# One queue slot earlier for half of one quad's attention weights, in a fused memory-attention and token-mixer kernel

## The chip, the cores and the metric

The kernel runs on one core of one Trainium2 chip. The metric is the device time of one execution in microseconds (us). Three runs of the kernel before gave 792.73, 793.41 and 793.94 us, a median of 793.41 us. PE is the matrix engine (TensorE; PEld its weight loads), DVE the vector engine, ACT the scalar engine, POOL is GpSimd, and SP is the engine whose queue issues the transfers.

## The reference

Eight batches, eight heads, 576 positions, head size 64, 32 memory slots. A softmax of `phi` pools keys and values into 32 slots per head, each query attends to these slots, and the result goes through a token mixer (576 to 256 to 576) and a channel mixer (512 to 1536 to 512), each with a residual:

```python
a = exp(phi - max(phi, axis=2)); a = a / (sum(a, axis=2) + 1e-9)   # over the 576 positions
k_m, v_m = einsum('bhsm,bhsd->bhmd', a, k), einsum('bhsm,bhsd->bhmd', a, v)
attn = softmax(q @ k_m^T / 8)                                       # over the 32 slots
x = (attn @ v_m) laid out as (batch, 576, 512)
u = x + (relu(x^T @ w_tok1) @ w_tok2)^T
out = u + relu(u @ w_ch1) @ w_ch2
```

Everything is float32. The kernel splits each operand of the large products into a high part in a rounded format (fp32r) and a low part, the rest, and adds three products, high by high, high by low and low by high.

## The kernel before

**Tiles and stages.** The four heads of half a batch are a *quad*; `Quad(b, Q)` names it by batch and half, so (2, 0) is the third batch's first quad. The channel mixer works on nine *chunks* of 512 of the 8 x 576 rows. A chunk has twelve pairs of products: the first (`cp`, line 159, twelve matmuls of 128x512) gives a block of 128 hidden channels, which ACT cuts at zero into a high part `hh` (line 126) and DVE completes with the low part `hl` (line 129); the second (`acc`, line 192, twelve matmuls) adds that block's part of the output. In the stage that matters here PE does `cp` of the next block and then `acc` of the block before it, over and over, and the attention of later batches is slipped in between.

**One quad's steps.** `load_phi`; `phi_max` (DVE reduces to `pr`, line 259, then POOL's all-partition maximum `prr`, line 270); `phi_exp` (DVE subtracts, line 273, ACT exponentiates, line 283); `phi_sum` (DVE line 259, POOL's all-partition sum `psr`, line 292); `step_kv` (`kvp`); `step_s` (scores `sp`); `sm2`, the softmax, whose end `sm3` sends the weights out and back by DMA as `raw`, transposes them into the tile `aT` and calls `a_pair(0)`; `a_pair(1)`; `nat` (`raw` into high and low parts); `v_pairs` (`vv`, line 484); `step_A` (`Ap`, then its parts `Ah` on ACT and `Al` on DVE); `step_R` (`Rp`, line 552, whose first matmul needs `Ah` and whose third needs `Al`); and `step_u` (`u`, line 573).

**The step that moves.** `a_pair(p)`, line 471, takes one half (64 of 128 partitions) of `aT`: ACT copies it to a high part (line 475), POOL subtracts for the low part (line 476). `v_pairs` puts its result `vv` in the same storage as `aT` (one buffer), so its first ACT copy cannot start before POOL has read the second half of `aT`. On ACT these stand behind each other: `vv`, `uh` (a chunk's left-over rows), `hh`, `Ah`.

**What sets the order.** Up to the end of chunk 0 a planner orders the steps. From there a table of events does: `at(h, fn, argument, k)` puts a call in slot h, sub-slot k (0 where none is given). For product number g the loop issues `cp` of g, then `run(2g-1, 1)`, then `hh` and `hl` of g, then `run(2g, 0)`, `acc` of the product before, `run(2g, 1)`, and `run(2g+1, -1, 0)`. Calls of one slot are issued in the order in which they were entered. The quad (2, 0), named `second`, has r = 24, so `sm2` stands in slot 27; the next quad, (2, 1), has its `phi_max` in slot 27 with k = 1, which the loop runs after slot 27's k = 0. Instructions of one engine run in the order in which they were issued.

POOL's `tensor_tensor` and its all-partition reductions run from different code libraries. Where one kind follows the other, the program holds an instruction between them that changes the library, shown as a bare `ISA` row in the listings below and as a `MODIFY_POOL_CONFIG` of POOL's queue in the trace.

Of the kernel before, what the change touches and what calls it, by code (L numbers as in the profile page):

```python
# [28 lines left out]
def kernel(  # L29
# [192 lines left out]
    def mixer(c):  # L222
        if c not in chunks:
            chunks[c] = Chunk(c)
        return chunks[c]
# [1033 lines left out]
    for Q, h0 in ((0, 3), (1, 11)):  # L1259
        qd = quads[1, Q]  # L1260
# [9 lines left out]
    second = ThirdBatchQuad(2, 0)  # L1270
# [34 lines left out]
    def at(h, fn, *x, k=0):  # L1305
        events.setdefault((max(h, 0), k), []).append((fn, x))

    beside = {}
    for b in range(2, B):
        for Q in range(2):  # L1310
            qd = second if b == 2 and not Q else Quad(b, Q)
            r = 2 * NF * b - (14 if Q else 26)
            if b == 2 and not Q:
                r = m = 2 * NF
            else:

                m = r - (0 if b == 2 else 10 if b > 3 or Q else 8)
                at(max(m - 11, 2 * NF), qd.load_phi)
                at(m - (6 if (b, Q) == (3, 0) else 7), qd.phi_max, k=1)
                at(m - 4, qd.phi_exp, k=1)  # L1320
                at(m - 3, qd.phi_sum, k=1)
                at(loaded + 1, qd.load_kv, k=1)
                at(r - 4, qd.load_q, k=1)
            loaded = m
            at(m, qd.step_kv)
            at(m + 4, qd.values)
            if b > 2:
                at(m + 3, qd.get_keys, k=1)
            else:
                at(m + 1, qd.step_T)  # L1330
            at(r + 2, qd.step_s)
            if Q or b == 2:
                at(r + 3, qd.sm2)
            else:
                beside[r + 3] = qd
            at(r + 4, qd.a_pair, 1)
            at(r + 6, qd.nat, k=1)
            at(r + 7, qd.v_pairs)
            at(r + 8, qd.step_A)
            at(r + 9, qd.step_R)  # L1340
            for x in range(4):
                at(r + 10 + x // 2 * (1 if qd is second else 2), qd.step_u, x // 2, x % 2)
        at(2 * NF * (b - 1) + 7, lambda b=b: mixer(b).take(), k=1)
    for c in range(CHUNKS):
# [6 lines left out]
        if h + 1 in beside:  # L1351
            qd = beside.pop(h + 1)
# [120 lines left out]
```

## Time and profile before

| what | number |
|---|---|
| median of 3 runs | 793.41 us (792.73 to 793.94) |
| the profiled execution's own time | 793.46 us |
| its span, first to last instruction | 791.6 us |
| PE busy | 765.9 us, 97% of the span |
| PEld busy | 638.3 us, 81% |
| DVE busy | 367.7 us, 46% |
| ACT busy | 246.4 us, 31% |
| POOL busy | 144.1 us, 18% |
| mean granted PE clock | 0.991 of full speed |

The span starts at 0 and all positions are in us from there; 1.86 us of the execution's time lie outside it. A row of a timeline gives the start, the duration, the engine, the line, the operation, output from input, the shape, the count, and in brackets how long the engine sat idle before and what ended it. Matmuls overlap: one is shown as lasting 0.39 us while the next starts 0.23 us after it. The changed lines are run once each, near 160 us of the 791.6.

### The profile page before, as it was taken

Reading aid. Unit: us, or ns where it says so; the run is one execution under the profiler, and the core shown is the slowest. Engines: PE = TensorE matmul, PEld = TensorE weight load, DVE = VectorE, ACT = ScalarE, POOL = GpSimd, SP = SyncE. Lnnn points to the kernel's source line nnn. Section 1 sums busy time; section 2 is a strip of 40 time slices with the busy share of each in tenths; the row PEclk is TensorE's granted clock in tenths of the full one; section 3 lists DMA queues with packets and bytes.
Section 4 is the critical chain, followed back from the end, with each engine's and each line's share of the span. In section 5 each row is a group of like instructions: output and inputs, shape, how many; then the busy total and the mean of one; then the engine's idle time right before and its main releaser. Section 6 shows DMA issues by size and latency. Waiting matters only on the chain.

```text
span 791.6 us, 11381 instructions
## 1 busy us (share of the span) xinstructions
PE 765.9 (97%) x4651; PEld 638.3 (81%) x4651; DVE 367.7 (46%) x640; ACT 246.4 (31%) x470; POOL 144.1 (18%) x124
## 2 busy tenths in 40 slices
PE   6799999978999999999999999999999999999998
PEld 5687878767787878788878888888878788888887
DVE  5989874434636444544344443536262422212113
ACT  3797664122322222232314232333233220210110
POOL 1344223010231013110221013101310402002000
PEclk9999999997999999999999999999999999999999
DMA  9916330141412312150406040504030101001001
GB/s 333 419 50 219 155 148 25 68 129 67 108 42 68 135 35 114 17 185 12 137 2 199 2 148 2 182 20 148 1 92 28 31 1 53 1 1 53 1 1 53
DMA packets 52243, 68.95 MB, mean 87 GB/s; under 512 B 33632, under 2 KB 42848, under 8 KB 47584
## 3 DMA queue, kind: packets, MB, share of 16 engines
q1 hardware_dynamic: 51616, 67.71, 25.6%
q8 instruction: 36, 0.59, 0.3%
q10 hardware_dynamic: 576, 0.52, 0.2%
q14 instruction: 15, 0.12, 0.1%
HBM read 54.92 MB, written 13.30 MB: 86 GB/s over the span
## 4 chain that ended last, share of the span: by engine, by line
PE 80%; DVE 10%; DMA 5%; issue 2%; ACT 2%; SPq 0%; POOL 0%; DVEq 0%; ACTq 0%; POOLq 0%
PE cp L159 34%; PE acc L192 32%; PE u L573 7%; DMA rawc<-in_w_ch_dram 3%; PE Ap L533 3%; DMA raww<-in_w_tok_tail_dram 2%; PE Rp L552 1%; DVE o L210 1%; PE end L192 1%; PE kvp L305 1%; DVE rawc L638 1%; DVE S L435 1%; DVE sm L430 1%; DVE S L411 1%; PE kvp L936 1%
## 5 line engine op out<-in xcount | busy, mean ns | idle before, releaser
L192 PE MATMUL acc<-hh,c 128*128 128x512 f32 x832 | 277.6, 394 | 0.8
L129 DVE SCALAR_TENSOR_TENSOR hl<-cp,hh 128x512 fp32r<-128x512 f32 x104 | 71.7, 690 | 278.9 <-ACT hh L126 278.8
L192 PEld LDWEIGHTS acc<-hh,c 128*128 128x128 f32 x832 | 156.2, 188 | 40.6 <-issue 6.5
L159 PE MATMUL cp<-uh,c1h 128*128 128x512 f32 x432 | 164.4, 394 | 0.0
L159 PE MATMUL cp<-ul,c1h 128*128 128x512 f32 x432 | 163.4, 392 | 0.0
L159 PE MATMUL cp<-uh,c1l 128*128 128x512 f32 x432 | 163.0, 391 | 0.0
L192 PE MATMUL acc<-hl,c 128*128 128x512 f32 x416 | 162.3, 390 | 0.0
L126 ACT ACTIVATE hh<-cp 128x512 fp32r<-128x512 f32 x104 | 62.0, 596 | 274.6 <-PE cp L159 274.6
L159 PEld LDWEIGHTS cp<-uh,c1l 128*128 128x128 f32 x432 | 81.6, 189 | 17.3
L159 PEld LDWEIGHTS cp<-ul,c1h 128*128 128x128 f32 x432 | 81.7, 189 | 16.6
L159 PEld LDWEIGHTS cp<-uh,c1h 128*128 128x128 f32 x432 | 81.1, 189 | 16.8 <-issue 0.4
L192 PEld LDWEIGHTS acc<-hl,c 128*128 128x128 f32 x416 | 78.2, 188 | 13.9
L476 POOL TENSOR_TENSOR a<-aT,a 64x576 fp32r<-64x576 f32 x24 | 34.3, 1428 | 217.8 <-ACT a L475 116.6
L204 POOL TENSOR_TENSOR o<-uh,ul 128x512 f32<-128x512 f32 x36 | 48.7, 1382 | 114.3 <-PE cp L159 46.9
L259 DVE TENSOR_REDUCE pr<-phi 128x128 f32<-128x640 f32 x27 | 35.4, 1315 | 15.2 <-ACT phi L283 8.1
L573 PE MATMUL u<-w2h,Rl 128*128 128x288 f32 x128 | 37.8, 295 | 0.2 <-DVE Rl L129 0.2
L573 PE MATMUL u<-w2l,Rh 128*128 128x288 f32 x128 | 37.8, 295 | 0.0
L573 PE MATMUL u<-w2h,Rh 128*128 128x288 f32 x128 | 37.7, 295 | 0.0
L475 ACT CAST a<-aT 64x576 fp32r<-64x576 f32 x24 | 16.2, 673 | 56.0 <-DVE aT L441 55.7
L533 PE MATMUL Ap<-w1h,nat 128*128 128x256 f32 x144 | 28.7, 291 | 0.7 <-DVE nat L983 0.7
L129 DVE SCALAR_TENSOR_TENSOR Rl<-Rp,Rh 128x512 fp32r<-128x512 f32 x16 | 11.1, 691 | 36.2 <-ACT Rh L126 36.2
L292 POOL PARTITION_ALL_REDUCE psr<-pr x11 | 11.9, 1082 | 73.8 <-issue 47.7
(156 smaller groups left out, 893.6 us busy)
## 6 DMA issues: line engine op xcount, KB each, us to landing
kv<-in_kv_dram SPq DMA_DIRECT2D x15, 1280.0 KB, 6.9
rawc<-in_w_ch_dram SPq DMA_DIRECT2D x12, 1024.0 KB, 9.8
q<-in_q_dram SPq DMA_DIRECT2D x16, 576.0 KB, 5.6
out_dram<-o SPq DMA_DIRECT2D x8, 1024.0 KB, 7.4
phi<-in_phi_dram SPq DMA_DIRECT2D x16, 320.0 KB, 4.1
rows<-S SPq DMA_DIRECT2D x48, 72.0 KB, 2.0
raw<-rows SPq DMA_DIRECT2D x12, 256.0 KB, 2.9
kv<-in_kv_dram SPq DMA_DIRECT2D x2, 640.0 KB, 12.1
```

The lines of the kernel that those rows point to most:

```text
L126: nc.scalar.activation(out=h, in_=ps, func=AF.Relu)
L129: nc.vector.scalar_tensor_tensor(out=l, in0=ps, scalar=0.0, in1=f32(h), op0=ALU.max, op1=ALU.subtract)
L159: nc.tensor.matmul(ps, l[:, a, w], r[:, a], start=n == 0, stop=n == len(mm) - 1)
L192: nc.tensor.matmul(ps, l_[f // 2][:, f % 2, a * P : (a + 1) * P], r[:, w], start=f == start and x == 0, stop=f == end - 1 and x == 2,)
L204: nc.gpsimd.tensor_tensor(out=s.o[:, a], in0=f32(s.uh[:, a]), in1=f32(s.ul[:, a]), op=ALU.add)
L210: nc.vector.tensor_tensor(out=o, in0=ps or s.acc[a], in1=o, op=ALU.add)
L259: nc.vector.tensor_reduce(out=m.rearrange("p (i m) -> p i m", i=4), in_=s.pt.rearrange("p i j m -> p i m j"), axis=AX.X, op=op,)
L292: nc.gpsimd.partition_all_reduce(s.r, m, P, RED.add)
L475: nc.scalar.copy(out=h, in_=s.aT[own])
L476: nc.gpsimd.tensor_tensor(out=l, in0=s.aT[own], in1=f32(h), op=ALU.subtract)
L533: nc.tensor.matmul(ps[:, :TT], a, w, start=x == 0, stop=x == len(mm) - 1)
L573: nc.tensor.matmul(ps[:, :HALF], a, r, start=x == 0, stop=x == len(mm) - 1)
```

## The change

`a_pair(1)` of the third batch's first quad goes from slot r + 4 to slot r + 3; all other quads keep r + 4. In slot r + 3 it stands directly behind `sm2`, which ends with `a_pair(0)`. It so comes ahead of `phi_max` of quad (2, 1) and ahead of `hh` and `hl` of the product in between.

```diff
@@ -1333,7 +1333,7 @@
                 at(r + 3, qd.sm2)
             else:
                 beside[r + 3] = qd
-            at(r + 4, qd.a_pair, 1)
+            at(r + (3 if qd is second else 4), qd.a_pair, 1)
             at(r + 6, qd.nat, k=1)
             at(r + 7, qd.v_pairs)
             at(r + 8, qd.step_A)
```

POOL's queue, from the residual of chunk 0 (`o`) to the sum of quad (2, 1). `a_2_0_1598` and `a_2_0_1599` are the two halves' tiles; the number behind `prr` and `pr` counts tiles and shifts by two:

```order
 L204 TENSOR_TENSOR o_1341<-uh_556,ul_557 128x512 x4
 L476 TENSOR_TENSOR a_2_0_1598<-aT_0_1596,a_2_0_1598 64x576
+L476 TENSOR_TENSOR a_2_0_1599<-aT_0_1596,a_2_0_1599 64x576
 L270 ISA
-L270 ISA prr_1_1619<-pr_1_1617 128x128
-L476 ISA
-L476 TENSOR_TENSOR a_2_0_1599<-aT_0_1596,a_2_0_1599 64x576
-L292 ISA
+L270 ISA prr_1_1621<-pr_1_1619 128x128
 L292 ISA psr_1_1702<-pr_1_1700 128x128
```

The second half's subtraction moves ahead of the maximum of the next quad. With it go two of the bare `ISA` rows, the one ahead of the second half (L476) and the one ahead of the sum (L292); POOL has two instructions fewer and all others as before.

ACT's queue, from the exponential of quad (2, 0)'s scores (`S`) to that of the next quad's `phi`:

```order
 L426 ACTIVATE S_0_1560<-S_0_1560 128x576
 L475 CAST a_2_0_1598<-aT_0_1596 64x576
-L126 ACTIVATE hh_1_1622<-cp_1_1604 128x512
-L350 CAST vh_0_1626<-vb_0_1507 128x256
 L475 CAST a_2_0_1599<-aT_0_1596 64x576
+L126 ACTIVATE hh_1_1624<-cp_1_1606 128x512
+L350 CAST vh_0_1628<-vb_0_1507 128x256
 L126 ACTIVATE hh_1_1657<-cp_1_1644 128x512
 L122 CAST nat_0_1673<-raw_0_1593 128x512
 L122 CAST nat_0_1673<-raw_0_1593 64x128
 L283 ACTIVATE phi_1_1509<-phi_1_1509 128x640
```

The second copy moves ahead of one `hh` and one `vh` copy, which each come one copy later. DVE, PE and SP keep their order, but for the numbers of tiles.

## The prediction

> **What bounds the kernel now.** I began with PE's busy share in the page, 97%, then asked the waits of PE, longest first. This is the first of them:
>
> ```profile
> PE 765.9 (97%) x4651; PEld 638.3 (81%) x4651; DVE 367.7 (46%) x640; ACT 246.4 (31%) x470; POOL 144.1 (18%) x124
> PE Rp L552 <- ACT Ah L122: 6.3, 1, 6.3
> ```
>
> PE is the bound, and in one place it stands for 6.3 us because `Ah` is late. The timelines of PE, ACT and POOL there say why:
>
> ```profile
> 173.55 0.39 PE L192 MATMUL acc<-hh,c 128*128 128x512 f32 x1
> 180.19 0.58 PE L552 MATMUL Rp<-vh,Ah 128*128 128x256 f32 x1 [6.26 <-ACT Ah L122]
> 181.10 0.58 PE L552 MATMUL Rp<-vh,Al 128*128 128x256 f32 x1
> 182.12 0.63 PE L159 MATMUL cp<-uh,c1h 128*128 128x512 f32 x1
> ...
> 169.30 0.74 ACT L283 ACTIVATE phi<-phi 128x640 f32<-128x640 f32 x1 [3.10 <-DVE phi L273]
> 177.54 1.22 ACT L484 CAST vv<-vh 64x128 fp32r<-64x128 f32 x4 [7.50 <-POOL a L476]
> 179.78 0.36 ACT L122 CAST Ah<-Ap 128x256 fp32r<-128x256 f32 x1
> ...
> 160.46 1.42 POOL L476 TENSOR_TENSOR a<-aT,a 64x576 fp32r<-64x576 f32 x1 [26.63 <-issue]
> 167.68 0.72 POOL L270 PARTITION_ALL_REDUCE prr<-pr  x1 [5.80 <-DVE nat L123]
> 176.12 1.39 POOL L476 TENSOR_TENSOR a<-aT,a 64x576 fp32r<-64x576 f32 x1 [7.71 <-issue]
> 183.32 1.09 POOL L292 PARTITION_ALL_REDUCE psr<-pr  x1 [5.82 <-PE Rp L552]
> ```
>
> POOL is idle 5.80, 7.71 and 5.82 us between a subtraction and a reduction: the changes of library. The second half waits for two of them, `vv` on ACT waits 7.50 us for it, `Ah` stands behind `vv`, and PE behind `Ah`. PE also comes back slowly. The chain shows the product behind the wait and a usual one, and the stretches of time show the clock (PEclk, behind the busy times; the last two columns are DMA share and GB/s):
>
> ```profile
> 182.32 4.91 PE cp L159 x12
> 214.58 2.72 PE cp L159 x12
> ...
> 26.41:29.82 3.41, 1.01 (x10) 0.82 (x9) 3.27 (x7) 2.82 (x5) 1.49 (x1) 1.00 1.02 420
> 29.82:33.23 3.41, 3.41 (x17) 3.18 (x17) 3.06 (x6) 3.41 (x6) 1.09 (x1) 0.50 1.00 406
> 50.30:53.71 3.41, 1.99 (x16) 1.80 (x15) 3.41 (x8) 3.06 (x6) 2.31 (x1) 1.00 0.00 0
> 173.18:176.59 3.41, 0.75 (x4) 0.29 (x2) 0.00 (x0) 0.00 (x0) 0.47 (x1) 1.00 0.00 0
> 176.59:186.83 10.24, 6.53 (x18) 5.17 (x19) 3.50 (x5) 3.16 (x8) 2.71 (x3) 0.50 0.00 0
> ```
>
> The clock fell to 0.50 for 10.24 us behind a stretch with PE busy 0.75 of 3.41 us, and earlier for 3.41 us behind one with 1.01; a stretch with 1.99 left it at 1.00. So the wait costs its own length and 4.91 - 2.72 = 2.19 us on the next product.
>
> **The change part by part.** *The second half.* It now follows the first on POOL. Such a pair takes 2.99 us in the next quad:
>
> ```profile
> 206.86 2.99 POOL L476 TENSOR_TENSOR a<-aT,a 64x576 fp32r<-64x576 f32 x2 [7.99 <-ACT a L475]
> 217.16 0.72 POOL L270 PARTITION_ALL_REDUCE prr<-pr  x1 [7.30 <-issue]
> 302.23 0.72 POOL L270 PARTITION_ALL_REDUCE prr<-pr  x1 [7.48 <-DMA kv<-in_kv_dram]
> 349.57 0.72 POOL L270 PARTITION_ALL_REDUCE prr<-pr  x1 [11.31 <-DVE Rl L129]
> 385.26 0.72 POOL L270 PARTITION_ALL_REDUCE prr<-pr  x1 [6.91 <-DMA kv<-in_kv_dram]
> 468.36 0.72 POOL L270 PARTITION_ALL_REDUCE prr<-pr  x1 [6.38 <-DVE pr L259]
> 553.05 0.72 POOL L270 PARTITION_ALL_REDUCE prr<-pr  x1 [7.47 <-DMA kv<-in_kv_dram]
> ```
>
> It ends at 160.46 + 2.99 = 163.45. The 7.71 us change of library is gone from the path of `vv`, and so is the 5.82 us one ahead of `psr`, which nobody waited for.
>
> *What is late next.* `vv` then no longer waits for POOL, but ACT still does the next quad's exponential ahead of it, and that waits for `prr`. `prr` needs one change of library, which now starts at 163.45 instead of 160.46 + 1.42 = 161.88. Before, the exponential ended at 169.30 + 0.74 = 170.04, which is 2.36 us after `prr` began. So `vv` starts at 163.45 + R + 2.36 = 165.81 + R, where R is the length of that change.
>
> *What R is.* Here before it was 5.80 us, and 5.82 us for `psr`. Where the queue had large loads in flight it was longer, as the rows above show: 7.30, 7.48, 6.91, 6.38 and 7.47, and at the longest 11.31. Starting later, it moves into such a load:
>
> ```profile
> 161.88:167.68 5.80, 5.80 (x27) 4.83 (x26) 1.96 (x4) 1.42 (x3) 0.00 (x1) 1.00 0.61 169
> 163.42:170.53 7.11, 7.11 (x37) 6.06 (x37) 2.95 (x5) 2.16 (x4) 0.72 (x1) 1.00 0.89 303
> 294.75:302.23 7.48, 7.48 (x41) 6.43 (x40) 3.97 (x6) 3.51 (x9) 0.00 (x1) 1.00 0.93 320
> 177.51:183.32 5.81, 3.02 (x9) 2.52 (x10) 3.14 (x5) 3.16 (x8) 0.00 (x0) 0.50 0.00 0
> 163.54 0.54 SPq L236 DMA_DIRECT2D phi<-in_phi_dram  x1
> 164.13 0.42 SPq L213 DMA_DIRECT2D out_dram<-o  x1
> ```
>
> The DMA engines were busy 0.61 of the old change and 0.89 of the time that the new one would take, near the 0.93 of the 7.48 us row. Neither `phi` nor the store moves. I take the mean of those five rows, (7.30 + 7.48 + 6.91 + 6.38 + 7.47) / 5 = 7.11 us, with 5.80 and 11.31 as bounds. The rows cannot tell whether a store delays it as a load does.
>
> The Trainium skill (GPSIMD Engine Reference, 2.1 Instruction dispatch) budgets about 6 us, 5.95 measured, for the first call after a library is loaded, whatever else runs. The trace agrees where the queue is empty (5.82) and not where it is busy (up to 11.31). By 5.95 the sum below would be 1.16 us larger.
>
> *PE.* `vv` starts at 165.81 + 7.11 = 172.92, 4.62 us earlier than 177.54. `uh`, `hh`, `Ah` and `Al` follow it as before, so `Rp` starts 180.19 - 177.54 = 2.65 us behind it at 175.57, and its third matmul 181.10 - 177.54 = 3.56 us behind at 176.48. At full clock `cp` follows that third matmul by 222.27 - 221.79 = 0.48 us:
>
> ```profile
> 221.79 0.28 PE L552 MATMUL Rp<-vh,Al 128*128 128x256 f32 x1
> 222.27 0.40 PE L159 MATMUL cp<-uh,c1h 128*128 128x512 f32 x1
> ```
>
> `cp` starts at 176.96 instead of 182.12: 5.16 us. PE is free at 173.55 + 0.23 = 173.78, so it still waits 1.79 us for `Ah` and, after 0.24 us of work, 0.67 us for `Al`. If the clock stays full, the product behind it saves 2.19 us.
>
> *What the moved copy delays.* ACT's second copy now stands ahead of `hh`, which comes one copy later, 160.24 - 159.66 = 0.58 us:
>
> ```profile
> 159.66 0.67 ACT L475 CAST a<-aT 64x576 fp32r<-64x576 f32 x1 [2.94 <-DVE aT L441]
> 160.24 0.59 ACT L126 ACTIVATE hh<-cp 128x512 fp32r<-128x512 f32 x1
> 160.86 0.69 DVE L129 SCALAR_TENSOR_TENSOR hl<-cp,hh 128x512 fp32r<-128x512 f32 x1
> 163.91 0.39 PE L192 MATMUL acc<-hh,c 128*128 128x512 f32 x1
> ```
>
> `hl` ends near 162.1 instead of 161.55, and `acc` needs it at 163.91: 1.8 us of cover, cost nothing. Without cover it would be 0.58 us. The low part of `v`, next on DVE, may wait for POOL until 163.45 and is first needed by `Rp`. The two library changes taken away cost nobody else: `psr` comes earlier. SP's order does not change.
>
> *Sum.* 5.16 + 2.19 = 7.35 us. Against the profiled execution's 793.46 that is 786.1 us; that execution stands 0.05 us over the median. Everything behind moves up together, since PE is busy from there to the end. If PE waited for nothing here, `cp` would start at 173.78 + 0.71 = 174.49 and the gain would be 9.82 us, the ceiling.
>
> **The rivals.** *The change of library is not stretched.* For it: the same place took 5.80 us with the first of these transfers in flight. `cp` then starts 1.31 us earlier: 784.8 us. By the skill's 5.95 it would be 784.9, and the same happens.
>
> *The clock falls all the same.* PE's two waits are 2.46 us together, so a stretch of 3.41 us that holds both has 0.95 us of work, which lies between the two rows that were followed by 0.50. A stretch that holds one of them has more. Where those stretches begin against the program is nothing I can set. It costs from half of 3.41 us, 1.7, to the 2.7 that the slow products cost before (2.19, and 182.12 - 181.10 - 0.48 = 0.54): 787.8 to 788.8.
>
> The Trainium skill (TensorE: Matmul & The Clock Gate, Part 1: The HAM clock gate) lets the clock fall after an idle window of about 3.4 us. The two rows with 1.01 and 0.75 us of work in it show that the window need not be quite idle. By the page alone a wait of 2.46 us keeps the full clock and 786.1 stands.
>
> *The change of library takes as long as the longest row.* With 11.31 us `vv` starts at 177.12, 0.42 before now, and the clock falls as before: 793.0, no change. Against it: in that row's place a load of keys and values and a store are both in flight; here only the store is.
>
> *Slower.* `vv` comes later than now if R exceeds 177.54 - 165.81 = 11.73 us, and each us more costs one. If the code waits for the store and for `q` behind it, half as much stretch again as in the longest row, R = 11.31 + (11.31 - 5.80) / 2 = 14.07, gives 793.46 + 2.34 = 795.8. No row is that long.
>
> *The move hides nothing.* POOL's order could keep `vv` waiting for another reason; the 7.50 us row names the second half alone.
>
> **How the numbers follow.** Chances: forecast, R of 6.4 to 7.5 at full clock, 0.42; not stretched 0.25; clock falls 0.23; longest row 0.05; slower 0.02; the move does nothing 0.03. The three cases that gain give 784.8, 786.1 and 787.8 to 788.8; the range from 784.5 to 788.8 holds them, with 0.1 left out. 0.2% is 1.6 us, about what a measurement can tell here. Faster 0.90, within 0.2% 0.08, slower 0.02.
>
> **What would show it.** On POOL two subtractions follow each other near 160.5 and `psr` follows without 5.8 us idle. ACT's wait of 7.50 us for POOL is gone, and `vv` starts with the end of the exponential, near 172.9. `Rp` waits about 1.8 us for `Ah` and the product behind it takes 2.7 us. It is wrong if the idle time ahead of `prr` exceeds 8 us, if that product takes 4 us or more, or if a new wait of PE appears at 163.9.

## The result, and the profile after

The changed kernel takes 785.09 us, the median of four runs (784.90 to 785.84); the kernel before takes 793.07 us (four runs, 792.16 to 793.94). The ratio is 0.9901, with a 95% interval of 0.9884 to 0.9918. The median fell by 7.98 us where 7.35 were forecast, and the time lies 1.0 us under the forecast and inside the range. The profiled execution took 785.84 us, the longest of the four; its span is 784.1 us.

The page's busy times, and the waits of PE from 155 to 180 us, after the change; they answer to the first two rows of the prediction:

```profile
PE 763.5 (97%) x4651; PEld 637.0 (81%) x4651; DVE 366.7 (47%) x640; ACT 247.8 (32%) x470; POOL 144.3 (18%) x124
```

```profile
PE Rp L552 <- ACT Ah L122: 1.1, 1, 1.1
PE Rp L552 <- DVE Al L123: 0.5, 1, 0.5
```

The wait for `Ah` is 1.1 us instead of 6.3, there is a small one for `Al`, and PE has no other in this stretch. The timeline of the same place after the change, POOL, ACT, DVE and PE in turn:

```profile
159.06 2.93 POOL L476 TENSOR_TENSOR a<-aT,a 64x576 fp32r<-64x576 f32 x2 [26.63 <-issue]
168.66 0.72 POOL L270 PARTITION_ALL_REDUCE prr<-pr  x1 [6.67 <-issue]
172.55 1.08 POOL L292 PARTITION_ALL_REDUCE psr<-pr  x1 [3.17 <-DVE pr L259]
...
158.25 1.38 ACT L475 CAST a<-aT 64x576 fp32r<-64x576 f32 x2 [2.94 <-DVE aT L441]
159.65 0.60 ACT L126 ACTIVATE hh<-cp 128x512 fp32r<-128x512 f32 x1
170.27 0.74 ACT L283 ACTIVATE phi<-phi 128x640 f32<-128x640 f32 x1 [5.72 <-DVE phi L273]
170.92 1.21 ACT L484 CAST vv<-vh 64x128 fp32r<-64x128 f32 x4
...
160.89 1.38 DVE L354 TENSOR_TENSOR vl<-vb,vh 128x256 fp32r<-128x256 f32 x1
...
172.13 0.39 PE L192 MATMUL acc<-hh,c 128*128 128x512 f32 x1
173.57 0.39 PE L552 MATMUL Rp<-vh,Ah 128*128 128x256 f32 x1 [1.05 <-ACT Ah L122]
174.61 0.45 PE L552 MATMUL Rp<-vh,Al 128*128 128x256 f32 x1 [0.53 <-DVE Al L123]
175.50 0.63 PE L159 MATMUL cp<-uh,c1h 128*128 128x512 f32 x1
```

The two subtractions now run as one pair; one change of library (6.67 us) is left ahead of `prr`; `psr` follows with no change of library; `vv` starts with the end of the exponential and waits for POOL no more. This execution reached the stage 1.41 us earlier than the one profiled before, since ACT's first copy starts at 158.25 instead of 159.66. That lead came about ahead of the changed place, and I take it off: `cp` starts at 175.50 instead of 182.12, which is 6.62 - 1.41 = 5.21 us earlier. The chain of waits and the stretches of time (PEclk behind the busy times) show the product behind it:

```profile
175.70 3.98 PE cp L159 x12
```

```profile
171.38:174.79 3.41, 1.83 (x9) 1.08 (x8) 2.99 (x5) 2.11 (x6) 1.08 (x1) 1.00 0.00 0
174.79:178.21 3.42, 3.42 (x11) 2.84 (x12) 1.63 (x2) 0.60 (x1) 0.70 (x1) 0.50 0.00 0
178.21:181.62 3.41, 3.41 (x23) 3.08 (x21) 1.11 (x2) 1.00 (x2) 0.00 (x0) 1.00 0.03 7
```

Here the clock still fell, for one stretch of 3.42 us instead of 10.24, and the product took 3.98 us instead of 4.91: 0.93 us saved where 2.19 were forecast. The gain between the two profiled executions is 5.21 + 0.93 + 1.41 = 7.55 of the measured 7.62 us, of which 6.14 belong to the change.

### The profile page after: what moved, and what is told of

Same layout as the page of the kernel before. It is cut to its first block, busy times and chain, and to the rows that moved or that the text cites. A ratio compares the mean times of both kernels' runs of the same rounds, so it can differ in the third digit from the quotient of the medians.

```text
span 784.1 us, 11378 instructions
## 1 busy us (share of the span) xinstructions
PE 763.5 (97%) x4651; PEld 637.0 (81%) x4651; DVE 366.7 (47%) x640; ACT 247.8 (32%) x470; POOL 144.3 (18%) x124
## 4 chain that ended last, share of the span: by engine, by line
PE 79%; DVE 10%; issue 6%; DMA 2%; ACT 1%; POOL 1%; SPq 0%; DVEq 0%; ACTq 0%; POOLq 0%
PE cp L159 33%; PE acc L192 31%; PE u L573 7%; PE Ap L533 3%; DMA kv<-in_kv_dram 1%; PE Rp L552 1%; DVE o L210 1%; DMA rawc<-in_w_ch_dram 1%; PE end L192 1%; PE kvp L305 1%; DVE rawc L638 1%; DVE S L411 1%; PE kvp L936 1%; DVE S L435 1%; DVE mx L418 1%
## 5 line engine op out<-in xcount | busy, mean ns | idle before, releaser
L476 POOL TENSOR_TENSOR a<-aT,a 64x576 fp32r<-64x576 f32 x24 | 34.3, 1431 | 209.5 <-ACT a L475 116.6
L292 POOL PARTITION_ALL_REDUCE psr<-pr x11 | 11.9, 1083 | 72.3 <-issue 48.1
```

Of the source, the lines that this page charges most:

```text
L292: nc.gpsimd.partition_all_reduce(s.r, m, P, RED.add)
L476: nc.gpsimd.tensor_tensor(out=l, in0=s.aT[own], in1=f32(h), op=ALU.subtract)
```

## The experiments

Theory: what cost the time was the change of library between the two halves, on the path from the second half over `vv` and `Ah` to `Rp`; the slow clock behind the wait was a cost of its own; and what is late next is `prr`, through the exponential that stands ahead of `vv`. The rivals: the place of ACT's copy was the cause; or the slow clock costs nothing; or something on POOL other than the change of library. Line numbers differ by a few between these kernels, since some add lines. The diffs of the first three runs are against the kernel before, the others against the changed kernel.

**1. The copy alone.** ACT's copy of the second half moves as in the change; POOL's subtraction stays where it was.

```diff
-        def a_pair(s, p):
+        def a_pair(s, p, parts=(0, 1), eng=None):
...
-            nc.scalar.copy(out=h, in_=s.aT[own])
-            nc.gpsimd.tensor_tensor(out=l, in0=s.aT[own], in1=f32(h), op=ALU.subtract)
+            if 0 in parts:
+                nc.scalar.copy(out=h, in_=s.aT[own])
+            if 1 in parts:
+                (eng or nc.gpsimd).tensor_tensor(out=l, in0=s.aT[own], in1=f32(h), op=ALU.subtract)
...
-            at(r + 4, qd.a_pair, 1)
+            if qd is second:
+                at(r + 3, qd.a_pair, 1, (0,))
+            at(r + 4, qd.a_pair, 1, (1,) if qd is second else (0, 1))
```

> Only ACT's copy of the second half moves up, as in the change; POOL's subtraction stays behind the next quad's maximum. If the gain comes from POOL's library changes (theory), nothing is gained: POOL still changes library twice more, ACT's vv still waits about 7.5 us and PE about 6.3 us for Ah, ratio 1.000 within 0.002. If it comes from ACT's new order (rival), most of the 1% gain is here: ratio 0.990 to 0.993.

Measured: 791.93 us against 792.90, ratio 0.9991 [0.9973, 1.0009]. The waits of PE, and the timeline of POOL and ACT:

```profile
PE Rp L554 <- ACT Ah L122: 5.9, 1, 5.9
```

```profile
174.96 1.39 POOL L478 TENSOR_TENSOR a<-aT,a 64x576 fp32r<-64x576 f32 x1 [7.54 <-issue]
176.38 1.22 ACT L486 CAST vv<-vh 64x128 fp32r<-64x128 f32 x4 [7.32 <-POOL a L478]
```

`vv` still waits 7.32 us for POOL's second half. The interval cannot tell the copy's gain from zero, so the change's gain lies with POOL's subtraction.

**2. The subtraction on DVE.** The order of before, but DVE does the second half's subtraction, so POOL changes its library once.

```diff
-        def a_pair(s, p):
+        def a_pair(s, p, eng=nc.gpsimd):
...
-            nc.gpsimd.tensor_tensor(out=l, in0=s.aT[own], in1=f32(h), op=ALU.subtract)
+            eng.tensor_tensor(out=l, in0=s.aT[own], in1=f32(h), op=ALU.subtract)
...
-            at(r + 4, qd.a_pair, 1)
+            at(r + 4, qd.a_pair, 1, nc.vector if qd is second else nc.gpsimd)
```

> The kernel before, but the second half's subtraction of the third batch's first quad is done by DVE in the old place, behind the next quad's maximum; the order of the calls is that of before. Theory (library changes are the cost): POOL needs no change back, vv starts at the end of the exponential near 170 us after a change of 5.8 us ahead of prr, Rp waits for nothing or under 0.3 us, and the clock stays full: the ceiling of the prediction, 9.8 us less than before, ratio 0.988. Rival (the place in the order is what counts): ratio 1.000.

Measured: 784.03 us (four runs, 783.00 to 784.93), ratio 0.9884 [0.9850, 0.9919]. The timeline of DVE, POOL and PE:

```profile
163.55 0.76 DVE L476 TENSOR_TENSOR a<-aT,a 64x576 fp32r<-64x576 f32 x1
...
168.84 0.72 POOL L270 PARTITION_ALL_REDUCE prr<-pr  x1 [5.61 <-DVE nat L123]
...
175.10 0.28 PE L552 MATMUL Rp<-vh,Ah 128*128 128x256 f32 x1
```

`Rp` starts with no idle time in front. With another remedy for the same cause the time falls nearly as far as the prediction's ceiling: 0.9884 of 793.41 is 784.2, a gain of 9.2 us where 9.82 was the ceiling.

**3. PE kept at work.** The order of before; 24 matmuls on constant data are added ahead of `Rp`, into the bank that `Rp` then overwrites. They fill most of the wait with work.

```diff
+            if s is second:
+                for _ in range(24):
+                    nc.tensor.matmul(
+                        ps.rearrange("p t n -> p (t n)"), c1h[:, 0, :P], chunks[1].uh[:, 0],
+                        start=True, stop=True,
+                    )
             s.mm_R(ps)
```

> The kernel before with 24 more matmuls of 128x512 on PE ahead of Rp of the third batch's first quad, into Rp's own bank, where Rp overwrites them; they take about 24 x 0.227 = 5.4 us of the 6.3 us wait. Theory (the half clock behind the wait is a cost of its own): the wait for Ah keeps its end, PEclk stays 1.00, Rp and the product behind it lose no time to the clock: 2.7 us less than before (2.19 + 0.54), ratio 0.9966. Rival (the clock costs nothing that counts): ratio 1.000.

Measured: 790.08 us (ten runs, 788.53 to 791.85), ratio 0.9962 [0.9944, 0.9979]. The timeline of POOL and ACT, and the chain of waits:

```profile
175.57 1.42 POOL L476 TENSOR_TENSOR a<-aT,a 64x576 fp32r<-64x576 f32 x1 [8.48 <-issue]
177.02 1.22 ACT L484 CAST vv<-vh 64x128 fp32r<-64x128 f32 x4 [8.29 <-POOL a L476]
```

```profile
181.33 2.73 PE cp L159 x12
```

`vv` comes as late as ever (PE still waits 1.4 us for `Ah` and 0.4 us for `Al` behind the added work), and still 0.0038 x 793 = 3.0 us are gone: the product behind `Rp` takes 2.73 us instead of 4.91. The wait and the slow clock behind it are two costs, and the second is near the 2.7 us that the prediction read off the rows.

**4. A reduction between the halves.** The changed kernel, with an added all-partition maximum of eight constant columns, whose result nobody uses, between the two halves. It goes into a new tile of 32 bytes for each partition.

```diff
+    def between():
+        t = wp.tile([P, 8], F32, tag="between", name="between", bufs=1)
+        nc.gpsimd.partition_all_reduce(t, ones[:, :8], P, RED.max)
...
+            if qd is second:
+                at(r + 3, between)
             at(r + (3 if qd is second else 4), qd.a_pair, 1)
```

> The changed kernel with one more all-partition maximum on POOL, of eight columns of a constant, between the two halves; it waits for no data and its result is not used. Theory (library changes): 5.8 us ahead of it and 7.7 us behind it come back, the second half ends near 160.5 + 1.4 + 5.8 + 0.7 + 7.7 + 1.4 = 177.5, vv waits for it as before, then one more change ahead of prr, which now also holds up the exponential ahead of vv: that ends near 177.5 + 5.8 + 2.4 = 185.7, about 8 us later than vv began before, so slower than before by about 8 us: ratio to before 1.010. Rival (the second half was late because the maximum ahead of it waited for its input): the constant is there from the start, ratio 0.990 as with the change.

Measured: 813.32 us (four runs), ratio 1.0255 [1.0219, 1.0290], far more than expected. In the stage itself nothing was unexpected: `Rp` waited 14.3 us for `Ah`. But twelve `cp` far from the stage took 2.80 us instead of 2.72, and so did twelve `acc`, as its chain of waits shows:

```profile
300.32 2.80 PE acc L192 x12
303.12 2.80 PE cp L159 x12
```

So the run did two things at once. The next one does the first alone.

**5. The same without a new tile.** The added maximum reads `ident` and writes into `ones`, a tile that is no longer needed then.

```diff
+    def between():
+        nc.gpsimd.partition_all_reduce(ones[:, :8], ident[:, :8], P, RED.max)
...
+            if qd is second:
+                at(r + 3, between)
```

> The changed kernel with one more all-partition maximum on POOL between the two halves, of eight columns of a constant, now into a tile that nobody reads any more, so that no tile is added and the layout of the memory stays that of the changed kernel. Theory (the library changes are the cost): PE waits about 14.3 us for Ah, as in the run before, and the whole is 8 to 10 us slower than before, ratio 1.011; the other 10 us of that run came from its added tile and are gone, matmul rows of 128x512 follow each other by 0.227 us again. Rival (those 10 us come from the library changes too): ratio 1.025 again.

Measured: 800.30 us against 792.35, ratio 1.0102 [1.0078, 1.0127]. Waits of PE, timeline of POOL, and the chain far from the stage:

```profile
PE Rp L552 <- ACT Ah L122: 14.6, 1, 14.6
```

```profile
159.87 1.42 POOL L476 TENSOR_TENSOR a<-aT,a 64x576 fp32r<-64x576 f32 x1 [26.64 <-issue]
167.66 0.39 POOL L1309 PARTITION_ALL_REDUCE ones<-ident  x1 [6.36 <-issue]
175.87 1.39 POOL L476 TENSOR_TENSOR a<-aT,a 64x576 fp32r<-64x576 f32 x1 [7.81 <-issue]
183.04 0.72 POOL L270 PARTITION_ALL_REDUCE prr<-pr  x1 [5.79 <-issue]
```

```profile
302.01 2.72 PE acc L192 x12
304.74 2.72 PE cp L159 x12
```

A reduction of 0.39 us on constant data makes the kernel 800.30 - 787.52 = 12.8 us slower than the changed kernel of the same comparison (run 8), near the 14.6 + 0.2 - 1.2 - 0.5 = 13.1 us by which PE waits longer (0.2 us is its wait for `Al` here, 1.2 and 0.5 us are the waits in run 8). Nothing waits for its result; what it brings is a change of library before it and one behind it, 6.36 and 7.81 us, and then one ahead of `prr`, 5.79, where the changed kernel has its only one. That is the cause by itself: not what the instructions wait for, but which library they need. The products far away are at 2.72 us again.

**6. The store later.** The changed kernel; the store of chunk 0, which was in flight during the change of library, goes six slots later.

```diff
-        at(h + 3, lambda c=c: chunks[c].store(), k=1)
+        at(h + (3 if c else 9), lambda c=c: chunks[c].store(), k=1)
```

> The changed kernel with chunk 0's store three products later (slot 33 instead of 27), so that the library change ahead of prr meets phi and q in the queue but no store. If the store stretches that change (theory): idle time ahead of prr falls from 6.67 to 5.6 to 5.9 us, vv comes about 0.9 us earlier, PE waits about 0.2 us for Ah and 0.5 for Al, the clock stays full: ratio to before 0.989. If it does not (rival): 6.67 us and the same waits as with the change, 1.05 and 0.53 us, ratio 0.9901.

Measured: 785.34 us (six runs, 784.00 to 786.86), ratio 0.9913 [0.9890, 0.9935]. The timeline of POOL, and the store's row in the queue of SP:

```profile
169.00 0.72 POOL L270 PARTITION_ALL_REDUCE prr<-pr  x1 [6.42 <-issue]
```

```profile
166.61 0.42 SPq L213 DMA_DIRECT2D out_dram<-o  x1
```

The change of library takes 6.42 us beside 6.67 and 6.80 in the two profiles of the changed kernel. But the edit delayed the store by less than was meant: it is issued 4.0 us into this change of library, which begins at 162.58, and so still meets its last 2.4 us; in the changed kernel it is issued after 0.7 us. The later store goes with a change that is 0.25 to 0.38 us shorter. What one without any store would take, this run does not show.

**7. The exponential behind `vv`.** The changed kernel; the next quad's `phi_exp` and `phi_sum` go two slots later, so that `vv`, `uh` and `Ah` stand ahead of the exponential on ACT.

```diff
-                at(m - 4, qd.phi_exp, k=1)
-                at(m - 3, qd.phi_sum, k=1)
+                late = (b, Q) == (2, 1)
+                at(m - (2 if late else 4), qd.phi_exp, k=1)
+                at(m - (1 if late else 3), qd.phi_sum, k=1)
```

> The changed kernel with the next quad's subtraction and exponential two products later, behind Ah and Al, and its sum likewise; vv no longer stands behind the exponential. Theory (what is late after the change is prr, through the exponential ahead of vv on ACT): Ah follows Ap at once, Rp waits for nothing, the clock stays full: the ceiling, 9.8 us less than before, ratio 0.9876. Rival (something else holds Ah, or the later exponential makes kvp wait): ratio 0.990 or above and a wait in front of kvp.

Measured: 783.00 us (six runs, 781.43 to 784.51), ratio 0.9881 [0.9861, 0.9902]. The timeline of POOL and ACT, and the chain:

```profile
168.82 0.72 POOL L270 PARTITION_ALL_REDUCE prr<-pr  x1 [7.58 <-issue]
...
164.67 1.22 ACT L484 CAST vv<-vh 64x128 fp32r<-64x128 f32 x4
169.08 0.37 ACT L122 CAST Ah<-Ap 128x256 fp32r<-128x256 f32 x1 [1.07 <-PE Ap L533]
```

```profile
171.79 0.71 PE Rp L552 x6
172.50 2.75 PE cp L159 x12
```

Here `prr` comes later than in the changed kernel (a change of library of 7.58 us), and no wait of PE is left at `Rp`: `Ah` now waits for PE, not PE for `Ah`. So the rest of the wait came from `prr` through the exponential, as the prediction said. 0.9881 of 793.41 is 784.0, 9.4 us under before. It is the lowest ratio measured, but its interval overlaps those of runs 2 and 10, so these three cannot be ranked.

**8. The changed kernel again**, beside the last two and the kernel before, for a comparison on one chip.

> The changed kernel again, for comparison on the same chip: ratio 0.990, with a wait of about 1 us for Ah and 0.5 us for Al, and in some executions a half clock of 3.4 us behind it, in others none.

Measured: 787.52 us (six runs, 784.73 to 787.97) against 792.35 us, ratio 0.9929 [0.9907, 0.9952]. It falls into two groups: 784.73 and 785.13 us with a mean granted clock of 0.997 and 0.999, and four from 787.45 to 787.97 with 0.988 to 0.996. The profiled one is of the second group; its stretches of time, and the product behind `Rp`:

```profile
173.47:176.88 3.41, 1.70 (x10) 1.07 (x9) 3.00 (x5) 1.57 (x4) 1.08 (x1) 1.00 0.00 0
176.88:180.29 3.41, 3.41 (x10) 2.66 (x9) 1.11 (x2) 0.60 (x1) 0.70 (x1) 0.50 0.00 0
```

```profile
176.89 4.35 PE cp L159 x12
```

With 1.70 us of work in 3.41 the clock fell again, and the product took 4.35 us. ACT's first copy starts at 159.66 in this execution, as in the one profiled before, so there is no lead to take off: it took 793.46 - 787.45 = 6.01 us less, near the 6.14 found above (whether the two ran on one chip is not on record). The interval shares 0.9907 to 0.9918 with that of the first comparison, so a gain of 6.5 to 7.4 us fits both, and it differs between executions. That the clock fell behind `Rp` in the four and not in the two is a guess: the slow product cost 4.35 - 2.72 = 1.63 us here, less than the 2.3 us or more between the groups, and where in an execution the clock fell is seen in the profiled ones alone.

**9. The tile alone.** The changed kernel with the 32-byte tile of run 4, set to zero by POOL in the same place, and no reduction.

```diff
+    def between():
+        t = wp.tile([P, 8], F32, tag="between", name="between", bufs=1)
+        nc.gpsimd.memset(t, 0.0)
...
+            if qd is second:
+                at(r + 3, between)
```

> The changed kernel with the added tile of 32 bytes per partition that the run with one more reduction had, only set to zero by POOL between the two halves, with no reduction and no library change. Theory (that tile shifts the tiles allocated after it, and PE's matmuls read them slower): matmuls of 128x512 follow each other by 0.232 us instead of 0.227, and the whole is 10 to 13 us slower than the changed kernel, ratio to before 1.003 to 1.008. Rival (the tile costs nothing, that run was slow for another reason): 0.227 us and ratio 0.990 to 0.993.

Measured: 797.60 us against 793.28, ratio 1.0056 [1.0038, 1.0074]. PE's groups by shape, and the chain of waits, at one place ahead of the stage and one behind it:

```profile
L192 PE MATMUL acc<-hh,c 128*128 128x512 f32 x832 | 280.9, 397 | 0.7
L159 PE MATMUL cp<-uh,c1h 128*128 128x512 f32 x432 | 165.6, 397 | 0.0
```

```profile
124.68 2.80 PE cp L159 x12
```

```profile
304.67 2.77 PE acc L192 x12
307.44 2.79 PE cp L159 x12
```

The waits at `Rp` are as in the changed kernel (0.96 and 0.54 us). Yet by the ratios it is slower than the changed kernel by 0.0155 x 793 = 12.3 us (against 0.9901) or 0.0127 x 793 = 10.1 us (against the 0.9929 of run 8), near what run 4 lost over run 5 (0.0153 x 793 = 12.1). `acc` and `cp` take 2.78 us for twelve matmuls instead of 2.72. The counts, 832 of which eight make an `acc` and 432 of which four make a `cp`, give 104 + 108 = 212 such groups, and 212 x 0.06 is 12.7 us. The means over all of these matmuls rose as well, to 397 ns from 394 and 393 on the changed kernel's page. At 124.68 us, long before POOL first writes the tile at 161.15, the product already takes 2.80 us (2.75 in the changed kernel). So the cost comes with the tile's being there and not with an instruction on it, and it falls on the products of the whole mixer.

**10. The loads later too.** The changed kernel, with the store as in run 6 and the load of a later `phi` behind that of `q`.

```diff
-                at(max(m - 11, 2 * NF), qd.load_phi)
+                at(m - 7 if (b, Q) == (3, 0) else max(m - 11, 2 * NF), qd.load_phi)
...
-        at(h + 3, lambda c=c: chunks[c].store(), k=1)
+        at(h + (3 if c else 9), lambda c=c: chunks[c].store(), k=1)
```

> The changed kernel with chunk 0's store three products later and the phi load of quad (3, 0) behind the q load, so that the library change ahead of prr meets only raw at its start and q at its end. Theory (transfers stretch it; the store alone took off 0.3 us): idle time ahead of prr 5.5 to 5.8 us, PE waits at most 0.1 us for Ah and 0.5 for Al, no half clock behind it, ratio to before 0.988 to 0.990. Rival (its length is its own, whatever the queue does): 6.4 to 6.8 us as before, and waits of 0.8 and 0.5 us.

Measured: 784.80 us (five runs, 781.91 to 785.70), ratio 0.9886 [0.9867, 0.9906]. The stretch between POOL's subtraction and `prr` (its length behind the colon, DMA share and GB/s last), in this run, in the changed kernel, in run 7 and in run 2, each in a fence of its own:

```profile
163.98:170.06 6.08, 6.08 (x29) 5.03 (x28) 1.95 (x4) 1.42 (x3) 0.00 (x1) 1.00 0.42 99
```

```profile
161.99:168.66 6.67, 6.67 (x34) 5.62 (x34) 1.95 (x4) 1.42 (x3) 0.00 (x1) 1.00 0.88 307
```

```profile
161.24:168.82 7.58, 7.58 (x42) 6.53 (x41) 3.34 (x6) 3.83 (x9) 0.00 (x1) 1.00 0.88 298
```

```profile
163.23:168.84 5.61, 5.61 (x26) 4.67 (x25) 2.71 (x5) 1.52 (x3) 0.00 (x1) 1.00 0.60 169
```

Here too both transfers come later without leaving the change of library: SP issues `phi` at 167.91 and the store at 168.37, ahead of its end at 170.06. With the DMA engines 0.42 busy instead of 0.88 it takes 6.08 us instead of 6.67, more than the 5.5 to 5.8 expected; PE waits 0.4 us for `Ah` and 0.5 us for `Al`, and the clock did not fall. Transfers may stretch it, but they don't set it alone: run 7 has the share of the changed kernel and takes 0.91 us more, and run 2 has more than this run and takes 0.47 us less. The runs don't tell what makes the rest.

## Why the prediction was right

**What bounds the kernel** was read rightly. PE's wait of 6.3 us was the change of library between the halves: the copy alone does nothing that its interval shows (run 1), the subtraction taken to another engine gives the same gain within the intervals (run 2), and a reduction between the halves with no data behind it takes it all away (run 5).

**The second half.** The pair was put at 2.99 us and took 2.93.

**What is late next** was `prr`, by way of the exponential ahead of `vv`; run 7 shows it.

**R** was put at 7.11 us and took 6.67. This term was mis-sized by 0.44 us, because I took it to be as long as in the rows with a large load in flight. Those five rows were a choice: nine changes of library ahead of a `prr` follow a pair in the trace before, and the four that are not in the mean (10.21 us at 264.87, 11.31 at 349.57, 11.05 at 432.91, 10.50 at 516.00) all have a load of keys and values and a store in flight. The mean of all nine is 8.73 us. Here a store and `phi` were in flight, without keys and values, and of the nine none had just these; that 7.11 came so near is in part luck. The prediction left open whether a store delays the change as a load does, and it stays open: in runs 6 and 10 the store, and in run 10 `phi`, came later but within the change, which then took 6.42 and 6.08 us. The lower bound, 5.80, was not reached in any run that keeps the pair on POOL. The Trainium skill (GPSIMD Engine Reference, 2.1 Instruction dispatch) has 5.95 us for the first call to freshly loaded code. The traces agree within 0.41 us where a single subtraction stands ahead (5.61 in run 2, 6.36 and 5.79 in run 5), and not behind the pair (6.08 to 7.58).

**PE's waits** were put at 1.79 for `Ah` and 0.67 for `Al`; they were 1.05 and 0.53. With R of 6.67 `cp` would have started 5.16 + 0.44 = 5.60 us earlier; it was 5.21, because it followed the third matmul of `Rp` by 175.50 - 174.61 = 0.89 us instead of 0.48, at half the clock.

**The product at full clock** is the step that failed in the profiled execution: 2.19 us were forecast, 0.93 were saved, and what happened there is the rival "the clock falls all the same". It cost 3.98 - 2.72 = 1.26 us on the product and 0.41 on `Rp`, 1.67 together, which is the lower end that the prediction gave it (1.7). The sign that the prediction named for full clock, a product of 2.7 us, did not come; with 3.98 us it lies just under the 4 us that were to show the prediction wrong, and in run 8's profiled execution, with 4.35 us, above them. The chance of 0.23 rested on two rows with 1.01 and 0.75 us of work in 3.41 ahead of a fall, and one with 1.99 us that kept the clock; here the clock fell behind 1.83 us, and in run 8 behind 1.70. How likely the fall is stays open: both profiled executions of the changed kernel had it, but the product took 2.77 us at full clock in run 6 (waits of 0.8 and 0.5 us) and 2.80 us in run 9 (0.96 and 0.54 us), where the tile alone makes it 2.80, and the busy time of the stretch ahead does not tell the cases apart (see the last section). The Trainium skill (TensorE: Matmul & The Clock Gate, Part 1: The HAM clock gate) asks for an idle window; in the two stretches ahead of a fall, here and in run 8, PE was busy for half of it.

**The cover of `hh` and `hl`** held: PE has no wait between 158 us and `Rp`. `vl` was held up beside POOL, as allowed for: it lasts 1.38 us in the timeline above instead of 0.70 us before, and ends 0.28 us after POOL's pair; nobody waited for it.

**The sum.** 786.1 forecast, less 0.44 for R, plus 1.67 for the clock, less the 1.41 by which this execution was ahead when it reached the stage, gives 785.9; the profiled execution took 785.84. So two mis-sized terms and an earlier start nearly cancel there, and that this execution came within 0.3 us of the forecast is luck. Without the lead the same sum gives 787.3, and run 8's profiled execution, which had none, took 787.45. The gain of the change alone in it is 6.14 us, and the medians give 7.98 in one comparison and 4.83 in the other (run 8). The forecast of 7.35 lies between them: the mechanism and the size of the main term held, and the clock behind them was left to chance.

## What to carry to other kernels

Count the changes of library between a producer and its consumer on POOL, and put instructions of one kind side by side; each such change near this stage took 5.5 us (run 3) to 8.6 us (run 4), with a reduction on constants as with one on data. When a wait is taken away, look at what stands ahead of the consumer on its own in-order engine: moving the next quad's exponential behind `vv` (run 7) took away what the change had left. Price the slow clock behind every gap of PE as a cost of its own, and keep the layout of memory the same in an experiment, since one new tile can move the time by more than the effect looked for.

## What was not expected of the hardware

**A tile of 32 bytes costs 10 to 12 us.** With it the 128x512 matmuls come every 2.78 / 12 = 0.232 us instead of 2.72 / 12 = 0.227, far from the place where the tile is used (runs 4 and 9 against run 5). It probably moves the tiles allocated behind it to other addresses; which tile's address matters was not tried.

**The clock can fall behind a stretch that is half busy.** In two profiled executions 1.83 and 1.70 us of work in 3.41 were followed by half the clock. The busy time of the stretch does not decide it alone. In run 5, with the stretches counted back from the place where the clock fell (178.34), one with 1.82 us was followed by one at full clock, though PE had nothing to do in that:

```profile
171.51:174.93 3.42, 1.82 (x9) 1.16 (x7) 0.00 (x0) 0.00 (x0) 0.00 (x0) 1.00 0.00 0
174.93:178.34 3.41, 0.00 (x0) 0.00 (x0) 0.00 (x0) 0.00 (x0) 1.39 (x1) 1.00 0.00 0
```

Run 1 has such a stretch with 1.86 us (from 171.29), and the changed kernel one with 1.67 us (from 778.95). What does decide is open.

**The way back takes longer.** The change from the reductions' library to that of the subtraction took 7.54 to 8.63 us in runs 1, 3, 4 and 5, the change the other way 5.54 to 7.58 us near the stage in all runs. In the rows that stand above the two kinds never ran with the same transfers. The trace before has both with the DMA engines almost idle: the way back took 6.78, 7.47 and 7.27 us (ahead of the `o` at 309.74, 393.45 and 561.04, DMA share at most 0.08), the other way 5.68, 6.26, 5.75 and 5.94 us (ahead of the `psr` at 321.04, 405.33, 487.57 and 572.60, DMA share 0.00). So the way back is longer without transfers too; why is not shown.
